# Pairs of row blocks in the last fold, one-row copies on ScalarE, even columns in the given order, and another order of the first blocks, in a spectral filter mixed with a token MLP

## The chip, the core and the metric

The kernel runs on one core of a Trainium2 chip. The metric is device time in microseconds: the median of three runs. Beside these runs, one execution was recorded by the hardware profiler, and all durations of single instructions come from that one. PE is the matrix engine, DVE the vector engine, ACT the scalar (activation) engine, POOL the GpSimd engine, and SP the engine that issues most of the DMAs. "L690" means line 690 of the kernel before.

## What is computed

The input `x` is 2048 rows of 512 bf16 numbers. Two branches are computed from it and mixed row by row with a gate:

```python
def _A_ref(x, w_r, w_i):            # spectral filter
    X = rfft2(x.astype(float32), axes=(-2, -1))
    X = X * (w_r + 1j * w_i)        # 2048 x 257 complex weights
    return irfft2(X, s=(S, D)).astype(bfloat16)

def _B_ref(x, w1, b1, w2, b2):      # MLP over the tokens
    h = _layernorm(x)               # over the 512 columns
    u = gelu(einsum("bsd,sf->bdf", h, w1) + b1)
    y = einsum("bdf,fs->bds", u, w2) + b2
    return y.transpose(0, 2, 1)

g = sigmoid((x * gate_w).sum(-1, keepdims=True))
return g * _A_ref(...) + (1 - g) * _B_ref(...)
```

The MLP has 2048 x 1792 weights each way. Both branches are matmuls in bf16: the transforms are products with tables of cosines and sines, split by radix-4 butterflies on DVE.

## The kernel before, in words

**Rows.** The 2048 rows are held as 16 blocks of 128. Block `j = 4q + r` is the rows `512q + 4a + r`, with `a` the partition. So `r` (0 to 3) is the row number modulo 4, and `q` the quarter.

**The MLP branch.** Layer norm of block `j`: `bn_stats` and `bn_aggr` on DVE (L471, L472), or for the blocks in `ASTAT` a sum and a sum of squares on ACT (L481, L485, into a shared scratch in `gl`); the root on ACT (L475); then either a reciprocal and a normalization on DVE (L495, L496, for the blocks in `OWN`) or a reciprocal and a product on DVE (L518, L519) and the normalization on ACT (L522). The first product (`m1`, L690) sums over all 16 blocks for each of 14 column tiles `ft` of `w1`: 224 matmuls of 512 columns. The first six tiles use the weights `wa`, block after block in the order `jorder`, as blocks become ready; the other eight use `wb` and need a free PSUM bank `acc`, which the GELU of an earlier tile frees (ACT, L704; a table load stands ahead of the first). The second product (`m2`, L966) makes one row block of the output from 14 matmuls. ACT (L986) scales it by `1 - g` into the output buffer; for the last two blocks DVE does it (L1004) with the addition.

**The filter branch.** For each `r`: butterflies over the quarters (`q4a`, `q4b`: L530, L531, L536, L537) give `xf`; PE transforms the rows (`fa`, four tasks per `r`, L547 to L550, table `ta`) into PSUM, with the even frequencies `0, 2, 4, ...` interleaved from two products, each written with a stride of two; ACT casts to `X` (L553); DVE does the first butterflies over the columns (`d4a`, `d4b`: L560 to L567). Then follow radix-4 butterflies over `r` (L586 to L599), the column transform (`fb`, L655 to L658) with casts to `B` (L662), the product with the filter on DVE (L805 to L831), the inverse butterflies, the inverse row transform (`i1`, L874 to L881) with casts (L887, L889) and folds (L897 to L910), and the inverse column transform (`i3`, L948 to L952). ACT scales its result by the gate into `eo` (L957). DVE folds `eo` (L971 to L975) and adds it to the output buffer (L992), block by block. Groups of blocks are stored by DMA.

**The filter's weights.** The filter needs each weight row and its mirror. The mirrored rows are loaded to `wt` and turned by a product with a permutation `flip` (`wf`, L742, cast at L746). A few rows that lie on no partition of their own are loaded to a strip (`wz`) and copied on partition 0 by five instructions of POOL per component (`special`, L445 to L449; components are the real and the imaginary part).

**The gate.** DVE multiplies `x` by `gate_w` (L715, four instructions, due number 6), ACT sums each block (L720, due number 5, 16 instructions); a tanh follows (L722) and DVE forms `g` and `1 - g`.

**The order.** Every piece of work is a task with an engine, an estimated duration, a due number (`prio`, a smaller one is more urgent), the tasks that it depends on, and buffers that it takes and frees. `Plan.order` simulates the engines with these estimates: whenever an engine is free it takes the most urgent task that is ready, a filler of low urgency too. Tasks are emitted in that order, and on the chip each engine runs its list strictly in order. A step on one engine depends on its predecessor on the same engine with a latency of 0.1 us in the plan. Loads are tasks of SP (or, for the first few, of ACT), with an estimate of their landing from bytes and packets. Loads that are issued before 6 us of the plan are counted 1.35 times as long.

Of the kernel before, what the change touches and what calls it, by code (L numbers as in the profile page):

```python
# [35 lines left out]
def make_tables():  # L36
# [10 lines left out]
    for r in range(4):  # L47
# [82 lines left out]
    flip = np.concatenate([np.eye(P)[::-1], np.eye(P)[(P - p) % P]], 1)  # L130
# [7 lines left out]
class Plan:  # L138
# [32 lines left out]
    def order(self):  # L171
# [17 lines left out]
        while events:  # L189
# [16 lines left out]
            while progress:  # L206
                progress = False
                for eng, ts in pending.items():
# [15 lines left out]
                    if best.pk:  # L224
# [4 lines left out]
                        dma_free = max(dma_free, issue + 0.8) + work / 16 * (1.35 if issue < 6.0 else 1.0)  # L229
# [25 lines left out]
def act(n, ptr=0):  # L255
    return 0.065 + 0.09 * ptr + n / 1200.0
# [12 lines left out]
def kernel(  # L269
# [25 lines left out]
    NEO, NES = 4, 2  # L295
# [49 lines left out]
    a0 = add("SP", 0.01, alloc_first, writes=["warm", "xs", "eps"], prio=-9)  # L345
# [34 lines left out]
    def ld_x0(q, eng, prio):  # L380
        ld([("x", 0, q)], lambda q=q: t["x"][:, q, 0, :], x4[:, q, 0, :], (P, 1024), prio, eng)
# [49 lines left out]
    def ld_W(comp, pr):  # L431
        v = wsrc[comp].rearrange("(e c k) l -> c e k l", e=4, k=4)
        z = wsrc[comp].rearrange("(e h q k) l -> h k q e l", e=4, h=2, k=2)
# [9 lines left out]
        def special():  # L443
            G, W, u, w = nc.gpsimd, t["W"], t["wt"], wz()
            G.tensor_copy(u[0:1, comp, 0, 0:2, 0:257], w[:, 5:8:2, 0:257])  # L445
            G.tensor_copy(u[0:1, comp, 0, 2, 0:257], w[:, 6, 0:257])
            G.tensor_copy(u[0:1, comp, 0, 3, 0:257], w[:, 0, 0:257])
            G.tensor_copy(W[0:1, comp, 0, 2:4, 0, 0:257], w[:, 1:4:2, 0:257])
            G.tensor_copy(t["wn"][:, comp, 0:257], w[:, 4, 0:257])  # L449
        add("POOL", 7.0, special, reads=[(k, comp) for k in ("wz", "u0", "u1", "w0", "w1")], writes=[("W", comp), ("wt", comp)], prio=0)  # L450
# [12 lines left out]
    OWN = {0: (0, 4, 8, 12), 1: (1, 5), 2: (2,), 3: ()}  # L463
    ASTAT = (8, 12, 5)
    QS, DP = 0.2, 4.9
    for r in range(4):
# [10 lines left out]
        for n, j in enumerate(OWN[r]):  # L477
            pj = 0.1 * n + ((-2.0, -2.0, -2.0, -1.8)[n] if r == 0 else 1.2 * r + 0.2 * n)
            if j in ASTAT:
# [7 lines left out]
                add("ACT", 0.6, asum, reads=[("x", r, j // 4)], writes=[("mvs", j), "ascr"], prio=-2 + 0.1 * n)  # L487
                add("ACT", 0.6, asq, reads=[("x", r, j // 4), ("mvs", j)], writes=[("mv", j), "ascr"], prio=-2 + 0.1 * n)
            else:
                add("DVE", 0.82, lambda j=j: stat(j), reads=[("x", r, j // 4)], writes=[("mv", j)], prio=pj)  # L490
            add("ACT", 0.28, lambda j=j: sq(t["rstd"][:, j:j + 1], t["mv"][:, j, 1:2], 1.0 / D if j in ASTAT else 1.0),
                reads=[("mv", j), "eps"], writes=[("rstd", j)], prio=-3)

# [4 lines left out]
            add("DVE", 0.55, nh, reads=[("mv", j), ("x", r, j // 4)], writes=[("rstd", j), ("h", j)], prio=pj - 0.05)  # L498
# [39 lines left out]
        pq = -1.75 if r == 0 else 1.2 * r + 1.2 + QS  # L538
# [3 lines left out]
        for dq in range(4):  # L542
            def fa(r=r, dq=dq):
# [3 lines left out]
                T.matmul(pa[:, 0, :, 0:P:2], lhsT=w(0), rhs=ta[:, 0:128], start=True, stop=True)  # L547
                T.matmul(pa[:, 0, :, 1:P:2], lhsT=w(1), rhs=ta[:, 128:256], start=True, stop=True)  # L548
# [123 lines left out]
    bt = add("PE", 0.3, biasT, reads=["b1", "b2", "flip"], writes=["pbias"], prio=10.096, alloc=["fa"])  # L672
# [7 lines left out]
    jorder = [4 * q + r for r in range(4) for q in range(4)]  # L680
# [32 lines left out]
    for r in range(4):  # L713
# [4 lines left out]
        for q in range(4):  # L718
            def ga(q=q, r=r):
                A.activation(t["x"][:, q, r, :], t["x"][:, q, r, :], ActF.Copy, accum_out=t["glog"][:, 4 * q + r:4 * q + r + 1])  # L720
            gates.append(add("ACT", act(512) + 0.1, ga, reads=xk, writes=[("xg", q, r)], prio=5))
# [217 lines left out]
    for grp in groups:  # L939
        for j in grp:  # L940
# [17 lines left out]
            add("ACT", act(512, 1), i3ev, reads=[("i3", j), "g"], writes=[("eo", j)], prio=1.5, alloc=["eo"], free=[tag])  # L958
# [11 lines left out]
            def fold(e, o, s):  # L970
                V.tensor_copy(s[:, :, :, 0], e[:, :, 0:129:128].rearrange("p h k -> p k h"))  # L971
# [4 lines left out]
            tfold = tiny(1) + 4 * tt(256)  # L976
            quart = lambda v: v.rearrange("p h (k d) -> p (h k) d", k=2)

            if j < LATE:
                def es(j=j, fold=fold, quart=quart):  # L980
                    s = sb([P, 2, 2, P], BF16, "es", NES)
                    fold(t["eo", j], quart(t["eo", j][:]), s)
                add("DVE", tfold, es, reads=[], writes=[("eo", j)], prio=4, alloc=["es"], free=["es"])

# [3 lines left out]
                add("ACT", act(512, 2), yev, reads=[("y", j, 0), "omg"], writes=[("o", j)], prio=1, free=["acc"], after=gates)  # L988

                def fin(j=j):  # L990
                    o = tbuf(j)
                    V.tensor_add(o, o, t["eo", j][:])  # L992
                add("DVE", tt(512), fin, reads=[("eo", j)], writes=[("o", j)], prio=4, free=["eo"])
            else:
                def es(j=j, fold=fold, quart=quart):
                    e, s = t["eo", j], sb([P, 2, 2, P], BF16, "es", NES)
                    V.tensor_scalar_add(e[:, 0, 0:129], e[:, 0, 0:129], t["ombb2"][:, j:j + 1])
                    fold(e, quart(tbuf(j)), s)
                add("DVE", tfold + 0.15, es, reads=[("eo", j), "omg"], writes=[("o", j)], prio=4, alloc=["es"], free=["eo", "es"], after=gates)
# [49 lines left out]
```

## Time and profile before

| what | value |
|---|---|
| median of three runs | 137.5 us (137.49 to 137.58) |
| the profiled execution | 137.48 us, of which its span is 135.6 us |
| granted PE clock in it | 0.993 |
| start of the first product (L690) on PE | 6.55 us |
| POOL's copies | 29.25 to 33.1 us and 38.78 to 43.1 us |
| DVE, 30 to 50 us | 9.93 us busy of each 10 |
| ACT, 30 to 40, 40 to 50, 50 to 60 us | 9.93, 9.68, 9.49 us busy |
| ACT, 70 to 80, 80 to 90 us | 1.46, 3.36 us busy |
| DMA engines | over 0.98 busy from 5 to 50 us, 328 to 388 GB/s |

The span runs from the first to the last instruction or transfer of the execution; the difference to its time lies around it. "Busy" counts what the profiler records of an instruction. The records of consecutive instructions overlap on an engine, so the distance between starts, not the recorded length, is what one costs in a stream. Idle time is put down to the instruction that released it.

### The profile page before, as it was taken

The page shows a single profiled execution, that of the slowest core. Times are in us where ns is not written, and L with a number is a line of the kernel's source. Part 1 is how long each engine was busy: PE and PEld are TensorE (multiplying, and loading weights), DVE is VectorE, ACT ScalarE, POOL GpSimd, SP SyncE. Part 2 cuts the span into 40 slices and gives each one's busy share as a digit, 9 for nine tenths or more (in the row PEclk, how much of TensorE's full clock was granted, in tenths as well). Part 3 has the DMA queues.
Part 4 walks back from the last instruction along what each step waited for, and adds up shares of the span by engine and source line. Part 5 has one row for each costly group of instructions (what it writes and reads, how often), then busy time and mean ns, then how long its engine had stood idle before and what let it go on. Part 6 is the DMA issues. An engine that isn't in the chain of part 4 may idle for free.

```text
span 135.6 us, 2193 instructions
## 1 busy us (share of the span) xinstructions
PE 127.0 (94%) x771; PEld 72.2 (53%) x771; DVE 118.1 (87%) x301; ACT 84.8 (63%) x175; POOL 8.4 (6%) x14
## 2 busy tenths in 40 slices
PE   6499999999999999999999899999999999999970
PEld 2146564654645457564445445555776575665660
DVE  2799989899999999819999999999659779999990
ACT  2976686699999999898111063222699377656400
POOL 0000000037057000000000000000000000000000
PEclk9999999999999999999999999999999999999997
DMA  4999999999999960980006900000000000321322
GB/s 119 342 342 369 355 374 348 336 299 344 332 324 405 407 267 0 286 337 0 0 0 221 400 0 0 7 0 2 0 0 0 5 0 0 155 114 48 155 77 80
DMA packets 17151, 23.22 MB, mean 171 GB/s; under 512 B 976, under 2 KB 14580, under 8 KB 17140
## 3 DMA queue, kind: packets, MB, share of 16 engines
q1 hardware_dynamic: 16564, 22.46, 48.8%
q10 hardware_dynamic: 576, 0.62, 1.5%
q8 instruction: 6, 0.10, 0.3%
q14 instruction: 5, 0.04, 0.1%
HBM read 20.97 MB, written 2.10 MB: 170 GB/s over the span
## 4 chain that ended last, share of the span: by engine, by line
PE 48%; DVE 36%; ACT 4%; DMA 4%; issue 3%; ACTq 1%; DVEq 0%
PE acc L966 19%; PE acc L690 16%; DMA wb<-in_B_w_dram 4%; PE fb L690 4%; DVE x L992 3%; DVE eo L974 3%; DVE es L973 3%; DVE st L560 2%; DVE X L561 2%; DVE es L972 2%; DVE eo L975 2%; DVE x L715 2%; DVE st L587 2%; DVE xp L586 2%; DVE X L567 2%
## 5 line engine op out<-in xcount | busy, mean ns | idle before, releaser
L966 PE MATMUL acc<-gl,wb 128*128 128x512 bf16 (+1 forms) x128 | 31.1, 373 | 0.4 <-DMA wb<-in_B_w_dram 0.4
L690 PE MATMUL acc<-h,wb 128*128 128x512 bf16 x128 | 30.0, 379 | 0.0
L986 ACT ACTIVATE x<-acc,ombb,omg 128x512 bf16<-128x512 f32 x14 | 10.8, 778 | 22.0 <-PE acc L966 22.0
L966 PE MATMUL acc<-gl,wa 128*128 128x512 bf16 (+1 forms) x96 | 24.2, 372 | 0.0
L966 PEld LDWEIGHTS <-wb 128*128 128x128 bf16 x136 | 14.8, 114 | 11.0 <-DMA wb<-in_B_w_dram 1.1
L690 PEld LDWEIGHTS <-wb 128*128 128x128 bf16 x128 | 12.5, 98 | 12.8
L690 PE MATMUL acc<-h,wa 128*128 128x512 bf16 x64 | 16.9, 379 | 1.9 <-DVE h L496 1.9
L966 PEld LDWEIGHTS <-wa 128*128 128x128 bf16 x102 | 11.4, 114 | 8.2
L690 PEld LDWEIGHTS <-wa 128*128 128x128 bf16 x96 | 9.4, 98 | 11.4 <-issue 1.8
L704 ACT ACTIVATE gl<-acc,b1f 128x512 bf16<-128x512 f32 x12 | 8.0, 694 | 6.1 <-PE acc L690 6.1
L553 ACT CAST X<-fa 128x512 bf16<-128x512 f32 x16 | 9.1, 586 | 2.9 <-PE fa L550 2.9
L471 DVE BATCH_NORM_STATS2 stats<-x 128x6 f32<-128x512 bf16 x13 | 8.8, 679 | 1.8 <-DMA x<-in_A_x_dram 1.7
L720 ACT ACTIVATE x<-x 128x512 bf16<-128x512 bf16 x16 | 10.0, 647 | 0.0
L690 PE MATMUL fb<-h,wa 128*128 128x512 bf16 x32 | 9.8, 379 | 0.0
L522 ACT ACTIVATE h<-x,nmr,rstd 128x512 bf16<-128x512 bf16 x9 | 7.1, 809 | 1.5 <-DVE nmr L519 1.5
L957 ACT ACTIVATE eo<-fa,g 128x512 bf16<-128x512 f32 x8 | 5.5, 685 | 2.7 <-DVE x L992 2.7
L957 ACT ACTIVATE eo<-fb,g 128x512 bf16<-128x512 f32 x8 | 5.5, 684 | 0.0
L662 ACT CAST B<-fa 128x512 bf16<-128x512 f32 x8 | 4.9, 618 | 0.8 <-PE fa L658 0.8
L992 DVE TENSOR_TENSOR x<-x,eo 128x512 bf16<-128x512 bf16 x14 | 5.3, 417 | 0.0
L715 DVE TENSOR_TENSOR x<-x,gw 128x2048 bf16<-128x2048 bf16 x4 | 5.2, 1312 | 0.0
L548 PE MATMUL fa<-rot,gl 128*128 128x128 bf16 x16 | 5.0, 312 | 0.1
L662 ACT CAST B<-fb 128x512 bf16<-128x512 f32 x8 | 5.0, 629 | 0.0
(177 smaller groups left out, 252.6 us busy)
## 6 DMA issues: line engine op xcount, KB each, us to landing
wb<-in_B_w_dram SPq DMA_DIRECT2D x8, 512.0 KB, 6.9
wb<-in_B_w_dram SPq DMA_DIRECT2D x4, 1024.0 KB, 6.1
wa<-in_B_w_dram SPq DMA_DIRECT2D x3, 1024.0 KB, 12.0
wa<-in_B_w_dram SPq DMA_DIRECT2D x2, 768.0 KB, 8.4
out_dram<-x SPq DMA_DIRECT2D x3, 512.0 KB, 2.6
x<-in_A_x_dram SPq DMA_DIRECT2D x2, 512.0 KB
wa<-in_B_w_dram SPq DMA_DIRECT2D x2, 384.0 KB
rot<-dft_ti SPq DMA_DIRECT2D x1, 736.5 KB
```

Source lines behind the costliest of these rows:

```text
L471: V.bn_stats(out=t["stats"][:, j, :], in_=t["x"][:, j // 4, j % 4, :])
L522: add("ACT", act(512, 2), lambda j=j: A.activation(t["h"][:, j // 4, j % 4, :], t["x"][:, j // 4, j % 4, :], ActF.Identity, bias=t["nmr"][ ...
L553: add("ACT", act(512), lambda r=r, dq=dq: A.copy(t["X"][:, :, r, :, dq, :], t["pa", r, dq][:]), reads=[("pa", r, dq)], writes=[("X", r, dq ...
L662: A.copy(t["B"][:, lt, e, 2 * c:2 * c + 2, :].rearrange("p s (i b) -> p s i b", b=4), t["pb", lt, e, c][:].rearrange("p s b i -> p s i b"))
L690: T.matmul(t["u", ft][:], lhsT=w[:, j // 4, j % 4, c * P:(c + 1) * P], rhs=t["h"][:, j // 4, j % 4, :], start=(j == jorder[0]), stop=(j == ...
L704: gelus.append(add("ACT", act(512, 1), lambda ft=ft: A.activation(t["gl"][:, ft, :], t["u", ft][:], ActF.Gelu_apprx_tanh, bias=t["b1f"][:, ...
L715: add("DVE", tt(2048), lambda r=r: V.tensor_mul(t["x"][:, :, r, :], t["x"][:, :, r, :], t["gw"][:, None, :].to_broadcast([P, 4, D])), read ...
L720: A.activation(t["x"][:, q, r, :], t["x"][:, q, r, :], ActF.Copy, accum_out=t["glog"][:, 4 * q + r:4 * q + r + 1])
L957: A.activation(t["eo", j][:], t["i3", j][:], ActF.Copy, scale=t["g"][:, j:j + 1])
L966: T.matmul(t["y", j, n][:, cs], lhsT=w[:, o, 512 * q + r:512 * q + 512:4], rhs=t["gl"][:, ft, cs], start=(ft == 0), stop=(ft == NFT - 1))
L986: A.activation(tbuf(j).rearrange("p h d -> p (h d)"), t["y", j, 0][:], ActF.Identity, bias=t["ombb2"][:, j:j + 1], scale=t["omg"][:, j:j + 1])
L992: V.tensor_add(o, o, t["eo", j][:])
```

## The change

The change has these parts.

- **Fold in pairs.** `eo` holds two blocks (two such buffers for four single ones). For the first 14 blocks, the fold (five instructions) and the addition to the output act on two blocks each. The last two blocks are folded singly as before.
- **One-row copies.** The five copies per component go from POOL to ACT, with due number 4.5. The two loads that held rows of the even frequencies, `u0` and `w0`, become four loads of 64 partitions each (`u0`, `u2`, `w0`, `w2`), four more loads in all.
- **Even columns.** The two products of L547 and L548 write 64 columns each, one after the other, in place of interleaved columns. The tables, `flip` and the loads of the filter follow that order.
- **First blocks.** `r = 0` goes through its blocks in the order 0, 8, 4, 12. The squares of block 8 on ACT wait for block 0's root; the statistics of block 4 on DVE wait for block 0's normalization. The table `ta` of `r = 0` is loaded by SP, after `w1`'s third piece, in place of ACT.
- **Numbers of the plan.** `QS` (the due number of the quarters' butterflies for `r > 0`) goes from 0.2 to -0.2, early loads are counted 1.2 times as long in place of 1.35, and some estimates of ACT grow.

```diff
-        k = 2 * p
+        k = 4 * (p % 64) + 2 * (p // 64)
...
-            sg = alt[:, None]
+            sg = np.where(p < 64, 1.0, -1.0)[:, None]
...
-    flip = np.concatenate([np.eye(P)[::-1], np.eye(P)[(P - p) % P]], 1)
+    flip = np.concatenate([np.eye(P)[::-1], np.eye(P)[np.where(p < 64, (64 - p) % 64, 191 - p)]], 1)
...
-                        dma_free = max(dma_free, issue + 0.8) + work / 16 * (1.35 if issue < 6.0 else 1.0)
+                        dma_free = max(dma_free, issue + 0.8) + work / 16 * (1.2 if issue < 6.0 else 1.0)
...
-    return 0.065 + 0.09 * ptr + n / 1200.0
+    return 0.11 + 0.09 * ptr + n / 1200.0
...
-    NEO, NES = 4, 2
+    NEO, NES = 2, 2
...
-    a0 = add("SP", 0.01, alloc_first, writes=["warm", "xs", "eps"], prio=-9)
+    a0 = add("SP", 0.6, alloc_first, writes=["warm", "xs", "eps"], prio=-9)
...
+    ld_w10(2, "SP", -8.8)
     ld_x0(3, "ACT", -8.8)
-    ld_ta(0, -8.78, "ACT")
-    ld_w10(2, "SP", -8.8)
     ld_w10(1, "SP", -8.7)
+    ld_ta(0, -8.65)
     ld_w10(3, "SP", -8.6)
...
-                ("u0", lambda: t["wt"][:, comp, 0, :, 0:257], z[1, 0], (512, 514)),
+                ("u0", lambda: t["wt"][0:64, comp, 0, :, 0:257], z[0, 1, 0], (256, 514)),
+                ("u2", lambda: t["wt"][64:128, comp, 0, :, 0:257], z[1, 1, 0], (256, 514)),
...
-                ("w0", lambda: t["W"][:, comp, 0, :, 0, 0:257], z[0, 0], (512, 514)),
+                ("w0", lambda: t["W"][0:64, comp, 0, :, 0, 0:257], z[0, 0, 0], (256, 514)),
+                ("w2", lambda: t["W"][64:128, comp, 0, :, 0, 0:257], z[1, 0, 0], (256, 514)),
...
-            G, W, u, w = nc.gpsimd, t["W"], t["wt"], wz()
-            G.tensor_copy(u[0:1, comp, 0, 0:2, 0:257], w[:, 5:8:2, 0:257])
...
-        add("POOL", 7.0, special, reads=[(k, comp) for k in ("wz", "u0", "u1", "w0", "w1")], writes=[("W", comp), ("wt", comp)], prio=0)
+            W, u, w = t["W"], t["wt"], wz()
+            A.copy(u[0:1, comp, 0, 0:2, 0:257], w[:, 5:8:2, 0:257])
...
+        add("ACT", 2.2, special, reads=[(k, comp) for k in ("wz", "u0", "u1", "u2", "w0", "w1", "w2")], writes=[("W", comp), ("wt", comp)], prio=4.5)
...
-    OWN = {0: (0, 4, 8, 12), 1: (1, 5), 2: (2,), 3: ()}
+    OWN = {0: (0, 8, 4, 12), 1: (1, 5), 2: (2,), 3: ()}
...
-    QS, DP = 0.2, 4.9
+    QS, DP = -0.2, 4.9
...
-            pj = 0.1 * n + ((-2.0, -2.0, -2.0, -1.8)[n] if r == 0 else 1.2 * r + 0.2 * n)
+            pj = (-2.0, -1.95, -1.9, -1.62)[n] if r == 0 else 1.2 * r + 0.3 * n
...
-                add("DVE", 0.82, lambda j=j: stat(j), reads=[("x", r, j // 4)], writes=[("mv", j)], prio=pj)
+                add("DVE", 0.82, lambda j=j: stat(j), reads=[("x", r, j // 4)], writes=[("mv", j)], prio=pj, after=[n0] if j == 4 else ())
...
+            if j == 0:
+                s0 = sj
+            if j == 8:
+                aq.deps.add(s0)
...
-        pq = -1.75 if r == 0 else 1.2 * r + 1.2 + QS
+        pq = -1.65 if r == 0 else 1.2 * r + 1.2 + QS
...
-                T.matmul(pa[:, 0, :, 0:P:2], lhsT=w(0), rhs=ta[:, 0:128], start=True, stop=True)
-                T.matmul(pa[:, 0, :, 1:P:2], lhsT=w(1), rhs=ta[:, 128:256], start=True, stop=True)
+                T.matmul(pa[:, 0, :, 0:64], lhsT=w(0), rhs=ta[:, 0:128], start=True, stop=True)
+                T.matmul(pa[:, 0, :, 64:P], lhsT=w(1), rhs=ta[:, 128:256], start=True, stop=True)
...
-    jorder = [4 * q + r for r in range(4) for q in range(4)]
+    jorder = [4 * q + r for r in range(4) for q in ((0, 2, 1, 3) if r == 0 else range(4))]
...
-                t["eo", j] = sb([P, 2, L], BF16, "eo", NEO)
-                A.activation(t["eo", j][:], t["i3", j][:], ActF.Copy, scale=t["g"][:, j:j + 1])
+                if j % 2 == 0:
+                    t["eo", j // 2] = sb([P, 2, 2, L], BF16, "eo", NEO)
+                A.activation(t["eo", j // 2][:, j % 2], t["i3", j][:], ActF.Copy, scale=t["g"][:, j:j + 1])
...
-                V.tensor_add(o[:, 0:4:3], s[:, :, 0], s[:, :, 1])
-                V.tensor_sub(o[:, 2:0:-1], s[:, :, 0], s[:, :, 1])
+                sv = s.rearrange("p k (j h) d -> p j h k d", h=2)
+                for u in range(o.shape[1]) if o.shape[1] == 1 else (slice(None),):
+                    V.tensor_add(o[:, u, 0:4:3], sv[:, u, 0], sv[:, u, 1])
+                    V.tensor_sub(o[:, u, 2:0:-1], sv[:, u, 0], sv[:, u, 1])
...
+                if j % 2 == 0:
+                    continue
...
+                def es(j=j, fold=fold, quart=quart):
+                    s, e = sb([P, 2, 4, P], BF16, "es", NES)[:], t["eo", j // 2]
+                    fold(e[:].rearrange("p j h d -> p (j h) d"), quart(e[:]), s)
+                add("DVE", tiny(1) + 4 * tt(512), es, reads=[], writes=[("eo", j - 1), ("eo", j)], prio=4, alloc=["es"], free=["es"])
 
                 def fin(j=j):
-                    o = tbuf(j)
-                    V.tensor_add(o, o, t["eo", j][:])
-                add("DVE", tt(512), fin, reads=[("eo", j)], writes=[("o", j)], prio=4, free=["eo"])
+                    tbuf(j)
+                    o = t["tb_"][:, j - 1:j + 1]
+                    V.tensor_add(o, o, t["eo", j // 2][:])
+                add("DVE", tt(1024), fin, reads=[("eo", j - 1), ("eo", j)], writes=[("o", j - 1), ("o", j)], prio=4, free=["eo"])
```

More of the change, by code (lines that the diff above doesn't have):

```diff
@@ L432, in ld_W @@
         v = wsrc[comp].rearrange("(e c k) l -> c e k l", e=4, k=4)
-        z = wsrc[comp].rearrange("(e h q k) l -> h k q e l", e=4, h=2, k=2)
+        z = wsrc[comp].rearrange("(e h i n k) l -> n h k i e l", e=4, h=2, n=2, k=2)
         wz = lambda: t["xp"][0:1, 2048 + 8 * WL * comp:2048 + 8 * WL * (comp + 1)].rearrange("p (j l) -> p j l", j=8)
@@ L497, in nh @@
                                 t["rstd"][:, j:j + 1], op0=Alu.add if j in ASTAT else Alu.subtract, op1=Alu.mult)
-            add("DVE", 0.55, nh, reads=[("mv", j), ("x", r, j // 4)], writes=[("rstd", j), ("h", j)], prio=pj - 0.05)
+            nj = add("DVE", 0.55, nh, reads=[("mv", j), ("x", r, j // 4)], writes=[("rstd", j), ("h", j)], prio=pj - 0.05)
+            if j == 0:
+                n0 = nj
         rest = [j for j in range(r, NJ, 4) if j not in OWN[r]]
@@ L720, in ga @@
                 A.activation(t["x"][:, q, r, :], t["x"][:, q, r, :], ActF.Copy, accum_out=t["glog"][:, 4 * q + r:4 * q + r + 1])
-            gates.append(add("ACT", act(512) + 0.1, ga, reads=xk, writes=[("xg", q, r)], prio=5))
+            gates.append(add("ACT", 0.72, ga, reads=xk, writes=[("xg", q, r)], prio=5))
     add("ACT", 0.3, lambda: A.activation(t["g"][:], t["glog"][:], ActF.Tanh, scale=0.5),
@@ L955, in i3ev @@
             def i3ev(j=j):
-                t["eo", j] = sb([P, 2, L], BF16, "eo", NEO)
-                A.activation(t["eo", j][:], t["i3", j][:], ActF.Copy, scale=t["g"][:, j:j + 1])
-            add("ACT", act(512, 1), i3ev, reads=[("i3", j), "g"], writes=[("eo", j)], prio=1.5, alloc=["eo"], free=[tag])
+                if j % 2 == 0:
+                    t["eo", j // 2] = sb([P, 2, 2, L], BF16, "eo", NEO)
+                A.activation(t["eo", j // 2][:, j % 2], t["i3", j][:], ActF.Copy, scale=t["g"][:, j:j + 1])
+            i3e = add("ACT", act(512, 1), i3ev, reads=[("i3", j), "g"], writes=[("eo", j)], prio=1.5, alloc=["eo"] if j % 2 == 0 else (), free=[tag],
+                      after=[i3e] if j % 2 else ())
             parts = [slice(0, D)] if j < NJ - 1 else [slice(0, L), slice(L, D)]
```

31 lines of the change are left out of this document (13 added, 18 removed).

## The prediction, made before the changed kernel ran

> **What bounds the kernel now.** I read the page first, then the chain of waits, then the timelines of PE, DVE, ACT and POOL, stage by stage. The page shows who is full:
>
> ```profile
> PE 127.0 (94%) x771; PEld 72.2 (53%) x771; DVE 118.1 (87%) x301; ACT 84.8 (63%) x175; POOL 8.4 (6%) x14
> PE 48%; DVE 36%; ACT 4%; DMA 4%; issue 3%; ACTq 1%; DVEq 0%
> ```
>
> PE has 94% of the span, and the chain runs over PE and DVE in turn. The PE timeline says more than the share: from its first product at 6.55 to its last at 131.21 it stands still for only about 1.4 us (0.27 at 48.99, 0.21 at 55.91, 0.36 at 75.98, the rest at 34 and 96.5). So the kernel is PE's list of matmuls, plus what lies ahead of 6.55, plus what follows 131.21. The second is set by a queue on ACT:
>
> ```profile
> 4.85 0.72 ACT L485 ACTIVATE gl<-x,mv 128x512 f32<-128x512 bf16 x1
> 5.48 0.19 ACT L485 ACTIVATION_READ_ACCUMULATOR gl<-x,mv 128x1 f32 x1
> 5.57 0.65 ACT L475 ACTIVATE rstd<-mv,eps 128x1 f32<-128x1 f32 x3
> 6.08 0.41 DVE L496 TENSOR_SCALAR h<-x,mv,rstd 128x512 bf16<-128x512 bf16 x1
> 6.55 1.02 PE L690 MATMUL acc<-h,wa 128*128 128x512 bf16 x4 [1.91 <-DVE h L496]
> ```
>
> Columns: start, us, engine and line. Block 0's statistics were complete at 4.36 (L472, 4.18 plus 0.18), but its root (L475) stands on ACT behind the squares of block 8 and starts at 5.57. The third part, the end:
>
> ```profile
> 130.17 1.04 PE L966 MATMUL fa<-gl,wb 128*128 128x256 bf16 x8
> 130.72 1.13 DVE L1004 SCALAR_TENSOR_TENSOR x<-acc,omg,x 128x512 bf16<-128x512 f32 x2
> 131.78 0.47 DVE L1004 SCALAR_TENSOR_TENSOR x<-fa,omg,x 128x256 bf16<-128x256 f32 x1
> ```
>
> The last product ends at 131.21, its addition starts at 131.78: DVE is 0.57 late, since it folds without a pause from 109.33 on. From 131.78 to the end of the span (0.47 and a store) lie 3.8 us, which stay.
>
> **The row transform (fa).** The change's edit to L547 and L548 is priced by two tasks of the same shape, one writing PSUM with stride two, one writing runs of 64:
>
> ```profile
> 10.22 0.27 PE L547 MATMUL fa<-rot,gl 128*128 128x128 bf16 x1
> 10.28 0.31 PE L548 MATMUL fa<-rot,gl 128*128 128x128 bf16 x1
> 10.39 0.31 PE L549 MATMUL fa<-rot,gl 128*128 128x256 bf16 x1
> 10.54 0.27 PE L550 MATMUL fa<-rot,gl 128*128 128x256 bf16 x1
> 10.65 0.27 PE L547 MATMUL fa<-rot,gl 128*128 128x128 bf16 x1
> ...
> 50.00 0.22 PE L655 MATMUL fb<-tb,X 128*128 128x128 bf16 x1
> 50.05 0.22 PE L656 MATMUL fb<-tb,X 128*128 128x128 bf16 x1
> 50.11 0.38 PE L658 MATMUL fb<-tb,X 128*128 128x256 bf16 x2
> 50.33 0.22 PE L655 MATMUL fa<-tb,X 128*128 128x128 bf16 x1
> ```
>
> Start to start the first takes 0.43, the second 0.33, each with two products of 128 columns and two of 256. The stride is the visible difference. There are 16 such tasks: 16 x 0.10 = **-1.6 us of PE** (bounds 0, if something else makes L547 slow, and -1.75, at 0.11 each).
>
> **The start.** ACT issues three loads in place of four (0.48 less, so the table load starts at 2.14, not 2.62), sums block 8 (0.70) and then does block 0's root before the squares. Its statistics, at 4.36, then decide: root at about 4.45, reciprocal 0.31 later as now (5.57 to 5.88), and 0.67 from reciprocal to PE as now (5.88 to 6.55): PE starts at 5.43, **-1.1 us** (bounds 0 and -1.3). Its weights are there: PE's weight load saw them at 4.65. Behind the waiting squares of block 8 stand the sums of block 12 and, on DVE, block 8's h. That h is ready at about 6.9 (squares end 5.6, root 5.9, DVE has block 4's statistics until 6.3), and PE asks for it at 5.43 + 6 x 0.22 = 6.75; block 4's h comes at 7.5 and is asked for at 8.2. The new wait of block 4's statistics for block 0's h is covered the same way. The table of the row transform goes to SP as its fifth load, ahead of the last quarter of weights; PE used the table at 10.22 and that quarter later than 9, both some 2 us after such a load lands.
>
> **What is given back.** PE gains 1.1 + 12 x 0.10 = 2.3 us by the time it has the first three quarters of the transform done, but h comes from DVE and ACT, which start no earlier. The tightest place is the last block:
>
> ```profile
> 29.60 0.82 ACT L522 ACTIVATE h<-x,nmr,rstd 128x512 bf16<-128x512 bf16 x1
> 30.44 1.28 ACT L704 ACT_TABLE_LOAD   x1
> 31.73 2.42 ACT L704 ACTIVATE gl<-acc,b1f 128x512 bf16<-128x512 f32 x4
> ```
>
> Its h ends at 30.42, the first bank is free at some 32.4, and PE starts the next column tiles at 32.67: 0.3 in hand. If these times stay, PE keeps only 0.2 us plus what it can do while it waits: the transform of the fourth quarter, now at 34.05 to 37.11 (4 x 0.43 and 0.34 of waiting). The new offset QS places that quarter's butterflies ahead of d4 (L560 to L567 at 27.47 to 30.16, 2.7 us), so its matmuls are there from about 29.5; and the third quarter's casts leave ACT earlier, so block 15's h may come 0.5 to 1 sooner. Bounds for what PE keeps of 2.75 us: 0.6 (gate unmoved, transform where it is: 0.2 and 4 x 0.10) and 2.75. I take **2.05**, 0.7 given back, nearer the upper end since both moves are in the code.
>
> **The tail.** A pair of blocks takes DVE 2.68 us now (L972 at 109.51 and 112.19 in the chain). Joined: the small copy 0.09, four operations of 512 elements at 0.34 (three steps from L899 to L903, 98.49 to 99.50) and the addition of 1024 at 0.60 (L591 to L592): 2.05 and some gaps, 2.1. Seven pairs save 4.1. DVE then ends its folds at 130.80 - 4.1 = 126.7 even if it starts no earlier, and PE ends at 131.21 - 2.05 = 129.16. So PE is the bound there by 2.5 us, and of the 0.57 a gap as between L671's end (24.59) and L675 (24.63) is left: **-0.5 us** (bounds 0 and -0.55).
>
> **The one-row copies.** On POOL they cost DVE time: while they run (29.25 to 33.1, 38.78 to 43.1) L567 takes 0.83 in place of 0.41, L560 1.10 and 0.88 in place of 0.68, L715 1.41 in place of 1.21. Adding these starts up, DVE loses about 2.7 us. On ACT no row shows them; between L755 (16 elements, 0.27) and L553 (512, 0.59) lie 0.4 for 257 elements and 0.6 for 514, so 2.4 us per component, bounds 1.4 and 2.9. ACT is full from 30 to 60, but 13 of the 16 gate sums (L720, 0.61 each) stand there with less urgent priority and need only be done by 79.23, where L986 first uses their result; ACT idles 22.0 us after 63. So on the path: 0. Without that cover it is 2.4 us on a cast of B. The 2.7 us of DVE is not counted either, PE being the bound; it is a reserve. Four more loads make SP later by 0.9 each; behind them stand the second wb load (used near 52, landed by 38) and w2, which waits 14.0 for PE anyway: 0. L715 fills DVE's pauses as before: 0.
>
> **The sum**: 137.48 (the profiled execution; 135.6 of span and 1.9 around it, the median being 137.5) - 2.05 - 0.5 = **134.9 us**.
>
> **Rivals.** *The gate holds.* PE keeps 0.6 of its lead: 137.48 - 0.6 - 0.5 = 136.4. For it: the 0.3 in hand, ACT and DVE full from 26 to 35. Against: the moved butterflies.
> *ACT waits for the filter.* Its queue is in order. If the copies stand ahead of h of block 7 (27.06), where ACT still has pauses, they wait for the rows (29.25 by POOL's start) and take 2.4; ACT goes on at 31.7 instead of 27.06, all behind it, the last h and the first bank, 4.6 later. PE fills 2.1 with the fourth quarter and had 0.3: 2.2 net on top of the lead lost, 137.48 + 2.2 - 0.5 = 139.2. It decides against the kernel when the block delays ACT by more than 2.9. Against it: the plan released L742 for 42.51 after 7 us booked for the copies, so it expects the rows after 32, later than they come, and ACT is then busy with more urgent work. The Trainium skill (SBUF — State Buffer, "Can I just issue two DMAs to hit both halves?") says that a transfer to 64 partitions reaches half the ports and that two of them serialize. The split loads would then take twice as long, an estimate from that page of 1.5 us more per component. No run here shows it; it would make this rival likelier and touch nothing else.
> *The plan shuffles away the gain.* Waits at the four places where PE stands still now grow by 2.5: 137.5.
>
> **Chances.** Forecast 0.70 (its own range 133.4 to 135.8), gate 0.16, ACT wait 0.08, shuffle 0.04, still faster than 133.4 by fewer waits 0.02. The low end is 137.48 - 2.75 - 0.55 - 0.8 (the three waits gone) = 133.4; the high end, 136.8, takes in the gate with 0.4 for a longer wait there. Some 0.2% (0.3 us) is what can be told from no change: faster 0.88, same 0.04, slower 0.08.
>
> **What would show it.** PE's first L690 near 5.4; the fa tasks at 0.33 each; no POOL copies and L567 at 0.41 throughout; a stop of PE of under 1 us between 28 and 33; folds in pairs of 2.1; the last addition within 0.1 of PE's end at about 129. A PE start after 6.2, fa tasks still at 0.43, or an ACT wait on the filter's loads ahead of the first L704 would prove the forecast wrong.

## The result, and the profile after

| | before | after |
|---|---|---|
| median of the runs | 137.5 us (137.46 to 137.58) | 135.7 us (135.34 to 136.38) |
| profiled execution; its span | 137.48; 135.6 | 136.38; 134.5 |
| first product of the MLP starts (L690, now L699) | 6.55 | 5.33 |
| last product of PE ends | 131.21 | 128.54 |
| first fold starts on DVE | 109.33 | 109.81 |
| last addition starts on DVE | 131.78 | 130.72 |

The ratio is 0.9875, 95% interval 0.9833 to 0.9916: faster by some 1.25%. The forecast was 134.9. The recorded execution is the slowest of its four, so what follows explains 136.38 and not the median. The table holds the main point: PE is done 2.67 us earlier, the last addition comes only 1.06 us earlier, and 1.06 is close to what the time lost (137.48 to 136.38, 1.1). Lines have moved: L690 is now L699, L966 is L977, L971 to L975 are L982 to L988, L992 is L1007, L1004 is L1019, L662 is L671.

The page of the changed kernel, busy times and the chain's shares:

```profile
PE 124.2 (92%) x758; PEld 70.9 (53%) x771; DVE 112.4 (84%) x259; ACT 88.9 (66%) x185; POOL 0.2 (0%) x4
...
PE 42%; DMA 28%; DVE 13%; SPq 8%; ACT 4%; issue 2%; DVEq 0%; ACTq 0%
```

PE has 2.8 us less work, DVE 5.7 less, ACT 4.1 more. DMA, which had 4% of the chain, has 28%. Most of that are loads of the MLP's weights and of the gate's row; 6% is the load of the filter's `w_i` rows into `W`, which ACT's copy at 45.16 (below) waits for. The start, in the timeline of all engines:

```profile
4.34 0.29 ACT L477 ACTIVATE rstd<-mv,eps 128x1 f32<-128x1 f32 x1
4.54 0.70 ACT L487 ACTIVATE gl<-x,mv 128x512 f32<-128x512 bf16 x1
...
4.87 0.41 DVE L503 TENSOR_SCALAR h<-x,mv,rstd 128x512 bf16<-128x512 bf16 x1
...
5.33 1.02 PE L699 MATMUL acc<-h,wa 128*128 128x512 bf16 x4 [0.59 <-DVE h L503]
```

Block 0's root now stands ahead of the squares of block 8. In PE's timeline, one row transform and the stops of over 0.25 us that come after the start (a row's time is where the stop ends):

```profile
8.37 1.02 PE L699 MATMUL acc<-h,wa 128*128 128x512 bf16 x4 [0.27 <-DVE h L503]
...
9.66 0.22 PE L556 MATMUL fa<-rot,gl 128*128 128x128 bf16 x1
...
9.99 0.22 PE L556 MATMUL fa<-rot,gl 128*128 128x128 bf16 x1
...
32.84 0.81 PE L699 MATMUL acc<-h,wb 128*128 128x512 bf16 x3 [0.38 <-ACT gl L713]
...
47.19 0.20 PE L761 MATMUL fa<-wt,flip 128*128 128x8 bf16 x2 [1.00 <-ACT W L755]
```

A task of the transform takes 0.33 (9.66 to 9.99). The stop at the first GELU bank (32.84) is 0.38. The largest stop, 1.00 up to 47.19, comes from ACT, whose timeline shows the one-row copies of the second component:

```profile
43.27 0.40 ACT L449 COPY wt<-xp 1x257 bf16<-1x257 bf16 x1
45.16 0.62 ACT L450 COPY W<-xp 1x514 bf16<-1x514 bf16 x1 [1.49 <-DMA W<-in_A_w_i_dram]
45.69 0.40 ACT L451 COPY wn<-xp 1x257 bf16<-1x257 bf16 x1
```

Five copies cost some 2.0 us a component, and here ACT also stands 1.49 us for a load: the rows of `w_i` in `W` landed near 45.1. In the kernel before POOL could start on all five copies at 38.78. The tables by stage show why, first of the kernel before, then of the one after (after the window: us, PE, PE loads, DVE, ACT, POOL, clock, busy share of the DMA engines, GB/s):

```profile
25.00:30.00 5.00, 5.00 (x32) 3.00 (x30) 4.38 (x14) 4.39 (x10) 0.75 (x2) 1.00 1.16 307
...
40.00:45.00 5.00, 5.00 (x29) 2.67 (x28) 4.93 (x8) 5.00 (x14) 3.10 (x3) 1.00 1.03 402
```

```profile
25.00:30.00 5.00, 5.00 (x30) 2.57 (x28) 4.72 (x15) 4.06 (x9) 0.00 (x0) 1.00 1.17 219
...
40.00:45.00 5.00, 5.00 (x25) 2.29 (x24) 4.90 (x17) 3.52 (x8) 0.00 (x0) 1.00 1.23 202
```

The DMA engines are at least as busy as before, and move 219 and 202 GB/s in place of 307 and 402 in two stretches in which the loads of 64 partitions run. Between them, from 35 to 40 us, such loads run too, and the rate is 298 in place of 314. The Trainium skill (SBUF — State Buffer, "Can I just issue two DMAs to hit both halves?") says that a pair of such transfers serializes, and that only one transfer over all 128 partitions reaches all the ports. The trace agrees in that the rate falls; no run here shows the ports.

The end, in the timeline of all engines:

```profile
127.50 1.04 PE L977 MATMUL fa<-gl,wb 128*128 128x256 bf16 x8
...
129.92 0.28 DVE L988 TENSOR_TENSOR x<-es 128x256 bf16<-128x256 bf16 x1
130.32 0.48 DVE L1019 SCALAR_TENSOR_TENSOR x<-acc,omg,x 128x256 bf16<-128x256 f32 x1
130.72 0.48 DVE L1019 SCALAR_TENSOR_TENSOR x<-fa,omg,x 128x256 bf16<-128x256 f32 x1
```

PE ends at 128.54; DVE is still folding at 130.2 and adds the finished product 2.18 us late (0.57 before). So DVE's path sets the end, and it has two idle stretches. The first, in DVE's timeline:

```profile
54.83 0.17 DVE L808 TENSOR_TENSOR ce<-cm 128x8 f32<-128x8 f32 x1
60.09 0.17 DVE L785 CAST c<-B 128x8 f32<-128x8 bf16 x1 [5.08 <-ACT B L671]
...
60.66 1.22 DVE L814 TENSOR_TENSOR xp<-B 128x2048 bf16<-128x2048 bf16 x1
```

DVE arrives 2.7 us earlier than before (55.0 against 57.7) and waits 5.08 us (2.66 before) for the casts of the even half of `B`. The same wait in the kernel before, in DVE's timeline:

```profile
60.33 0.17 DVE L776 CAST c<-B 128x8 f32<-128x8 bf16 x1 [2.66 <-ACT B L662]
```

DVE takes that half first, and ACT casts it last: the odd half was complete at 53.65. DVE's work on that half thus starts at 60.66, against 60.91 before, and the first fold no earlier than before. The second idle stretch lies among the folds. The tables of the stage from the first fold to the last addition, before and after:

```profile
109.33:131.78 22.45, 21.87 (x158) 13.88 (x155) 21.82 (x99) 12.04 (x19) 0.00 (x0) 1.00 0.21 83
```

```profile
109.81:130.72 20.91, 18.62 (x138) 12.17 (x138) 18.76 (x57) 11.28 (x18) 0.00 (x0) 1.00 0.24 95
```

DVE's busy time fell by 3.06 (21.82 to 18.76), the stage by 1.54: idle time grew from 0.63 to 2.15. The waits of DVE and of ACT from 105 us on (us in total, times, longest):

```profile
DVE es L982 <- ACT eo L967: 4.3, 3, 2.7
```

```profile
ACT eo L967 <- DVE x L1007: 4.1, 4, 2.1
```

The longest of DVE's three waits, 2.7, ends with the first fold and so lies ahead of the stage; the other two, 0.79 each, lie in it. Each engine waits for the other. `eo` has two buffers, of two blocks each; a buffer comes free only when both its blocks are added, and the next fold needs both of its blocks there.

### The profile page after: what moved, and what is told of

Its sections match the earlier page's. It is cut to its first block, busy times and chain, and to the rows that moved or that the text cites. A ratio compares the mean times of both kernels' runs of the same rounds, so it can differ in the third digit from the quotient of the medians.

```text
span 134.5 us, 2134 instructions
## 1 busy us (share of the span) xinstructions
PE 124.2 (92%) x758; PEld 70.9 (53%) x771; DVE 112.4 (84%) x259; ACT 88.9 (66%) x185; POOL 0.2 (0%) x4
## 4 chain that ended last, share of the span: by engine, by line
PE 42%; DMA 28%; DVE 13%; SPq 8%; ACT 4%; issue 2%; DVEq 0%; ACTq 0%
PE acc L977 21%; PE acc L699 12%; DMA wa<-in_B_w_dram 9%; SPq L310 8%; DMA gw<-in_gate_w_dram 8%; DMA W<-in_A_w_i_dram 6%; DMA wb<-in_B_w_dram 4%; ACT eo L967 3%; DVE eo L987 2%; DVE es L984 2%; DVE x L1007 2%; DVE es L983 2%; DVE eo L988 2%; PE fb L883 1%; PE fb L667 1%
## 5 line engine op out<-in xcount | busy, mean ns | idle before, releaser
L977 PE MATMUL acc<-gl,wb 128*128 128x512 bf16 (+1 forms) x124 | 30.8, 372 | 0.2
L699 PE MATMUL acc<-h,wb 128*128 128x512 bf16 x124 | 28.6, 379 | 0.5 <-ACT gl L713 0.4
L977 PE MATMUL acc<-gl,wa 128*128 128x512 bf16 (+1 forms) x94 | 23.9, 372 | 0.1
L977 PEld LDWEIGHTS <-wb 128*128 128x128 bf16 x136 | 15.1, 114 | 10.7 <-DMA wb<-in_B_w_dram 0.8
L699 PEld LDWEIGHTS <-wb 128*128 128x128 bf16 x128 | 12.5, 98 | 14.0 <-DMA W<-in_A_w_r_dram 0.7
L699 PE MATMUL acc<-h,wa 128*128 128x512 bf16 x61 | 16.9, 379 | 1.0 <-DVE h L503 0.9
L977 PEld LDWEIGHTS <-wa 128*128 128x128 bf16 x102 | 11.3, 114 | 8.0 <-issue 0.2
L699 PEld LDWEIGHTS <-wa 128*128 128x128 bf16 x96 | 9.3, 98 | 9.9 <-issue 1.2
L699 PE MATMUL fb<-h,wa 128*128 128x512 bf16 x32 | 9.4, 379 | 0.0
L982 DVE COPY es<-eo 128x8 bf16<-128x8 bf16 (+1 forms) x9 | 1.6, 182 | 4.4 <-ACT eo L967 4.3
L477 ACT ACTIVATE rstd<-mv,eps 128x1 f32<-128x1 f32 x16 | 4.7, 296 | 0.5 <-DVE rstd L527 0.4
L671 ACT CAST B<-fa 128x512 bf16<-128x512 f32 x8 | 4.8, 598 | 0.3 <-PE fa L667 0.3
L671 ACT CAST B<-fb 128x512 bf16<-128x512 f32 x8 | 4.8, 601 | 0.0
```

Source lines behind the costliest of these rows:

```text
L671: A.copy(t["B"][:, lt, e, 2 * c:2 * c + 2, :].rearrange("p s (i b) -> p s i b", b=4), t["pb", lt, e, c][:].rearrange("p s b i -> p s i b"))
L699: T.matmul(t["u", ft][:], lhsT=w[:, j // 4, j % 4, c * P:(c + 1) * P], rhs=t["h"][:, j // 4, j % 4, :], start=(j == jorder[0]), stop=(j == ...
L977: T.matmul(t["y", j, n][:, cs], lhsT=w[:, o, 512 * q + r:512 * q + 512:4], rhs=t["gl"][:, ft, cs], start=(ft == 0), stop=(ft == NFT - 1))
```

## The experiments

All times are medians. The runs of a1 to b1, of the c's and of the d's were made on three chips, each time beside runs of the kernel before on the same chip, whose median was 137.58 to 137.65. The ratio to these, with its 95% interval, is formed from the runs and is not the quotient of the medians. "Changed kernel" is the one after. Times of single instructions come from one recorded execution of each kernel.

**a1_single_folds.** The changed kernel with the old folds, one block at a time, and four buffers.

```diff
-    NEO, NES = 2, 2
+    NEO, NES = 4, 2
...
-                t["eo", j // 2] = sb([P, 2, 2, L], BF16, "eo", NEO)
+                t["eo", j] = sb([P, 2, L], BF16, "eo", NEO)
...
-                add("DVE", tiny(1) + 4 * tt(512), es, reads=[], writes=[("eo", j - 1), ("eo", j)], prio=4, alloc=["es"], free=["es"])
+                add("DVE", tfold, es, reads=[], writes=[("eo", j)], prio=4, alloc=["es"], free=["es"])
```

> The changed kernel with the last fold and the addition undone to one block per instruction and four single buffers; all else as changed (135.7 us). Theory (the pairs brought little: with two pair buffers DVE and ACT wait for each other, 5.2 us for two pairs against 5.36 for four single blocks before): 135.5 to 136.3, DVE without pauses from the first fold to the last. Rival (the pairs carry much of the gain, 4.1 us of DVE time being saved at the end): 137 or more.

Measured: 138.21 us (137.17 to 139.23), ratio 0.9999 (0.995 to 1.0048). PE's last product ends at 128.72, the last addition starts at 131.76, where it started before. The rival held: PE's 2.5 us alone are worth nothing, and without the pairs the change shows no gain.

**a2_copies_on_pool.** The one-row copies back on POOL.

```diff
-            A.copy(u[0:1, comp, 0, 0:2, 0:257], w[:, 5:8:2, 0:257])
+            nc.gpsimd.tensor_copy(u[0:1, comp, 0, 0:2, 0:257], w[:, 5:8:2, 0:257])
...
-        add("ACT", 2.2, special,
+        add("POOL", 7.0, special,
```

> The changed kernel with the ten one-row copies back on POOL. Theory (the wait of ACT for the second component's rows, 1.49 us in the profile, costs PE 1.0 us and delays B, and it is this that scatters the runs over 1 us): ACT has no such wait and the runs scatter less; but POOL takes back up to 2.7 us of DVE time ahead of B, so 135 to 136. Rival (the copies on ACT are free and DVE's time counts): 136.5 or more. The rows would still land at about 45, so the turning products still wait for them.

Measured: 137.55 us (137.09 to 138.03), ratio 0.9957 (0.9916 to 0.9998). The last addition starts at 132.22, 1.50 later than in the changed kernel, and PE stops for 1.65 us up to 49.09, for DVE's `X`. POOL's copies of the second component start at 44.00 and not at 38.78 as before, beside the split loads, which are still there. The rival held here too: DVE's loss, set down as a reserve, counts. What POOL's copies cost with whole loads, this run doesn't show.

**a3_whole_loads_stride_two.** Row transform, tables and loads of the filter as before the change: the stride of two and whole loads.

```diff
-                ("u0", lambda: t["wt"][0:64, comp, 0, :, 0:257], z[0, 1, 0], (256, 514)),
-                ("u2", lambda: t["wt"][64:128, comp, 0, :, 0:257], z[1, 1, 0], (256, 514)),
+                ("u0", lambda: t["wt"][:, comp, 0, :, 0:257], z[1, 0], (512, 514)),
...
-                T.matmul(pa[:, 0, :, 0:64], lhsT=w(0), rhs=ta[:, 0:128], start=True, stop=True)
+                T.matmul(pa[:, 0, :, 0:P:2], lhsT=w(0), rhs=ta[:, 0:128], start=True, stop=True)
```

> The changed kernel with the even columns as before (products written with a stride of two, loads of 128 partitions, old tables). Theory (loads to 64 partitions run at half the rate): the second component's rows land at 38 to 41 and not at 45, ACT does not wait for them, PE does not stop at 47; the row transform takes 0.43 a task again, 1.7 us more of PE. Net 135.5 to 136.5 with a scatter of under 0.4. Rival (the split loads cost nothing, the lateness has another cause): rows still at 44 to 45, and 137 or more.

Measured: 136.23 us (136.1 to 137.12), ratio 0.9876 (0.9807 to 0.9945): no difference from the changed kernel that these intervals could show. PE's last product ends at 128.66 (128.54) and the last addition starts at 130.84 (130.72). ACT does not wait in the copies and PE does not stop near 47. What the runs of 64 columns give PE, the split loads that come with them take back. In this kernel the DMA engines move 301 GB/s from 25 to 30 us and 390 from 40 to 45, which ties the loss of rate to the split (c3, with the split loads, moves 240 and 265). Its runs lie 1.0 us apart, where under 0.4 was expected, so the split loads are not all that scatters the runs.

**b1_interleave_in_cast.** Both at once: a3 with runs of 64 columns in PSUM, interleaved by ACT's cast, so that the loads stay whole. (The cast turns the odd columns too; the table `ta` holds these in an order that makes up for it.)

```diff
-                T.matmul(pa[:, 0, :, 0:P:2], lhsT=w(0), rhs=ta[:, 0:128], start=True, stop=True)
+                T.matmul(pa[:, 0, :, 0:64], lhsT=w(0), rhs=ta[:, 0:128], start=True, stop=True)
...
-lambda r=r, dq=dq: A.copy(t["X"][:, :, r, :, dq, :], t["pa", r, dq][:]),
+lambda r=r, dq=dq: A.copy(t["X"][:, :, r, :, dq, :].rearrange("p l c (i n) -> p l c i n", n=2), t["pa", r, dq][:].rearrange("p l c (n i) -> p l c i n", n=2)),
```

> As the run with whole loads, but the two products are written one after the other and ACT's cast to X puts the even columns in order (it reads PSUM in pairs of columns 64 apart). Loads of 128 partitions, copies on ACT. Theory (stride costs PE 1.65 us, split loads cost about 1 us): 134.0 to 135.0, row transform 0.33 a task, rows at 38 to 41, scatter under 0.4, faster than both the changed kernel and the one with the stride. Rival (the end hangs on DVE's fold and not on PE): within 0.4 of the run with the stride. Should the cast slow down by the strided reading, its 16 instructions show it (0.58 now).

Measured: 135.67 us (135.44 to 135.77), ratio 0.9819 (0.9757 to 0.9881). PE's last product ends at 128.07, the last addition starts at 130.25, 2.18 later, as in the changed kernel and in a3: DVE is the bound, as the rival had it. But the time meets neither forecast: it is 0.56 below that of a3, where the rival said within 0.4, and above the range of the theory. Against a3 PE ends 0.59 earlier (not 1.65: it came to its full rate later, see the last section, and stops 0.37 at the first GELU bank, where a3's does not), the even half of `B` is complete some 0.5 earlier, the first fold starts 0.59 earlier (109.34 and 109.93), and so does the last addition. What PE gains ahead of `B` does reach the end here, through the casts that DVE waits for.

**c1_swap_halves, c4_before_swap.** DVE takes the odd half of `B` first, which ACT has cast first: in the changed kernel (c1) and in the kernel before (c4).

```diff
-    for lt in range(2):
-        pr = 3.2 + 0.1 * lt
+    for lt in (1, 0):
+        pr = 3.3 - 0.1 * lt
```

> The changed kernel with one loop turned round: the filter product takes the odd half (lt = 1) before the even one. Nothing else. Theory (the end hangs on DVE's path, not on PE: DVE stands still for 5.08 us at 55 to 60 because the even half of B, which it takes first, is cast last, though the odd half lies ready): the pause shrinks to under 1 us, the last fold starts 4 us earlier, near 105.5, DVE's folds end ahead of PE, and the end follows PE's last product (128.5) by some 4 us: 134.2 for the profiled execution, 133.5 to 134.5 in the median, against 135.7. Rival (PE is the bound already, the 2.2 us between PE's end and the last addition are the work of the last two blocks): within 0.4 of the changed kernel.

> The kernel before with only the loop turned round. Theory (two bounds lay almost level before: PE ends at 131.2, DVE's folds let the last addition start at 131.78): DVE's pause of 2.66 us goes, the folds end ahead of PE, the end follows PE: 0.4 to 0.6 less, 136.9 to 137.2. Rival (DVE alone was the bound): 1.5 us or more less. Second rival (PE alone): nothing.

Measured: c1 134.16 us (132.85 to 135.16), ratio 0.9686 (0.9593 to 0.9779); c4 136.77 us (136.48 to 138.02), ratio 0.9926 (0.9881 to 0.9972). In c1 the work on `B` starts at 56.67, the first fold at 106.90 (109.81), and the last addition starts 0.03 after PE's end, at 130.35. The recorded execution took 135.16, 1.0 over the median: ACT waited 2.2 us for the `w_i` rows and PE 2.25 us. In c4 the first fold is at 106.80, 2.53 earlier, and the last addition 0.04 after PE's end (132.56). The swap takes DVE off the path in both. In the kernel before DVE was only 0.57 late, so PE, the other bound, lets little of the 2.53 through; the time came out somewhat below the theory's. The recorded execution of c4 took 138.02, and its PE ends 1.35 later than in the kernel before, since it came late to its full rate (last section); it shows which engine waits, and the median what the swap is worth.

**c2_interleave_and_swap, c3_three_pair_buffers.** b1 with the swap (c2); the changed kernel with a third buffer for the pairs, and one for the folded sums to make room (c3):

```diff
-    NEO, NES = 2, 2
+    NEO, NES = 3, 1
```

> Whole loads, contiguous products, even columns put in order by the cast, and the loop turned round as in the run before it. Theory: PE's last product ends at 128.1, as without the turned loop, and the end is 0.1 + 3.8 behind it: 133.3 to 134.0, faster than every kernel so far and steadier. Rival (another wait takes over once the pause is gone, the single row that goes through DRAM-side loads and PE ahead of the inverse transform): 134.5 to 135.5.

> The changed kernel with three buffers for pairs in place of two (and one scratch of the fold in place of two, to make room). Theory (two buffers make ACT and DVE wait for each other, 4.1 us and 1.6 us of pauses in the fold phase): from the first fold to the last addition 19.0 to 19.6 in place of 20.9, 134.3 to 135.0. Rival (the pauses of ACT are only where it has nothing to do, since PE's i3 products are placed late by the plan): 20.5 or more, no change.

Measured: c2 133.87 us (133.44 to 133.94), ratio 0.969 (0.9622 to 0.9757), the last addition 0.03 after PE's end. c3 134.33 us (133.93 to 134.5, and one run of 139.01), ratio 0.9721 (0.9616 to 0.9826). The table of c3's fold stage:

```profile
109.07:128.47 19.40, 18.49 (x140) 12.18 (x138) 18.68 (x57) 11.17 (x18) 0.00 (x0) 1.00 0.24 96
```

DVE has the same work as in the changed kernel (18.68 and 18.76) in 1.5 us less; the last addition comes 0.35 after PE's end. So the mutual waits were the buffers' doing. The rest of c3's lead in this record is another thing: the `w_i` rows landed in time (copy L450 at 43.76, without a wait), PE does not stop near 47, the even half of `B` is ready 0.88 earlier (59.69 and 60.57) and the first fold starts 0.74 earlier than in the changed kernel.

**d3_old_start, d2_interleave_swap_old_start.** The old order of the first blocks and loads, with the estimates that went with it, in the changed kernel (d3), whose end hangs on DVE, and in c2 (d2), whose end hangs on PE.

```diff
-    OWN = {0: (0, 8, 4, 12), 1: (1, 5), 2: (2,), 3: ()}
+    OWN = {0: (0, 4, 8, 12), 1: (1, 5), 2: (2,), 3: ()}
...
-            if j == 8:
-                aq.deps.add(s0)
```

> The changed kernel with the old order of the first blocks, first loads and block 0's root and nothing else. Theory: its end hangs on DVE, which has a wait of 5.1 at B's even half: PE's last product ends near 129.7 (128.54 in the changed kernel), but the last addition starts at 130.4 to 131.0 (130.72), time 135.4 to 136.1. Rival: what starts earlier ends earlier: last addition near 131.8, time 136.6 to 137.0.

> The interleaving cast and the swapped halves, with the old order of the first blocks, first loads and block 0's root. Theory: PE is the bound there, so its start counts in full: first product of the MLP at 6.55, PE's last product near 129.7, last addition within 0.1 of it, time 134.8 to 135.2 (133.87 with the new start). Rival: the end hangs on DVE there too: 133.7 to 134.2.

Measured: d3 135.49 us (135.18 to 135.57), ratio 0.9817 (0.975 to 0.9883); PE starts at 6.54 and ends at 129.22, and the last addition starts at 130.51. The earlier start shows no gain in the changed kernel, as its theory had it. PE's lead of 1.21 is 0.68 at the end; the stops of 0.27 and 0.38 are not there in d3. The `w_i` rows come into it as well: ACT and PE wait for them in both records, they landed 0.34 earlier in d3 (copy L450 at 44.82), and the even half of `B` was ready 0.34 earlier (60.23). d2 134.17 us (134.14 to 135.8), ratio 0.9763 (0.9664 to 0.9863), 0.3 more than c2 and not the 1.1 of its theory. The time lies in the rival's range, but not for the rival's reason: the last addition starts 0.04 after PE's end (128.82). The two recorded executions differ in more than the start: c2's PE lost 0.8 us by coming late to its full rate (last section), and d2's stops 0.79 us up to 31.15 for a cast, where c2's stops 0.18. What the earlier start is worth where PE is the bound stays open.

**d4_swap_single_folds, d1_interleave_swap_three_buffers.** The two changes to the folds again where PE is the bound: a1 with the swap (d4), c2 with c3's buffers (d1). Their edits are those above.

> The changed kernel with the halves swapped and the old folds, one block at a time. Theory: the first fold comes near 107 and the folds take 22.5, so DVE is done at 129.5 to 130.3, level with PE: time 134.1 to 134.9, and the pairs, worth 2.5 without the swap, are worth at most 0.7 with it. Rival: the pairs are worth 2.5 wherever z comes: 136.4 to 136.9.

> The interleaving cast, the swapped halves and three pair buffers together (one buffer of the folded sums in place of two, for room). Theory: with the halves swapped PE is the bound at the end, so a shorter fold phase is worth nothing: PE's last product ends at 128.3 to 128.8 and the last addition starts within 0.1 of it, time 133.5 to 134.2, the same as with two buffers (133.87). Rival: the waits between DVE and ACT in the folds also hold PE back through the banks of the last products: PE's last product at 127.8 or earlier, time 132.5 to 133.2.

Measured: d4 133.13 us (132.62 to 134.06), ratio 0.9657 (0.9579 to 0.9735); d1 133.47 us (133.42 to 133.5), ratio 0.9674 (0.9609 to 0.9739). The end of d4, in the timeline of all engines:

```profile
126.80 1.04 PE L975 MATMUL fa<-gl,wb 128*128 128x256 bf16 x8
127.88 0.48 DVE L1013 SCALAR_TENSOR_TENSOR x<-fa,omg,x 128x256 bf16<-128x256 f32 x1 [1.04 <-PE fa L975]
```

DVE waits 1.04 us for PE there, with single folds; the first fold had started at 103.66. The forecast of 107 came from c1, whose record holds the wait of 2.2 us for the `w_i` rows; here that wait is 0.19. The time lies 1.0 under the theory's range. The pairs, without which the gain was nil in a1, bring nothing that shows once the halves are swapped, and in d1 the third buffer adds nothing that the intervals show. Both kernels beat the changed one and the one before.

## Why the prediction was right in part

**Right.** The start (5.43 forecast, 5.33), the row transform (0.33 a task), and what is given back at the gate: PE was to end at 129.16 and ended at 128.54, with a stop of 0.38 where under 1 was forecast. No POOL copy is left to slow DVE. The first rival, the gate, had the right place (the second set of column tiles starts at 32.84, 32.67 before) and too high a price. That the time fell into the range is in part luck: the forecast had the wrong engine at the end, and PE's term, which came to nothing, was made up in part by a tail that gave twice its forecast.

**The step that failed** is in the tail: "DVE then ends its folds at 130.80 - 4.1 = 126.7 even if it starts no earlier", and from it "PE is the bound there by 2.5 us". The folds ended at 130.2. The size of a pair was nearly right (two pairs and one wait of 0.79 take 5.18, from 117.25 to 122.43, so 2.19 each, 2.1 forecast, which makes 0.6 in seven pairs), but DVE's work in the stage fell by 3.06 and not 4.1, two buffers gave 1.52 of that back as mutual waits (c3 gets that back), and the first fold came 0.48 later, as it needs two blocks of `eo` where it needed one (109.29 with single folds in a1). Sum: 0.48 - 3.06 + 1.52 = -1.06, the shift of the last addition.

**What had been overlooked** is the wait for `B`, 2.66 us, which stood in the trace of before. All that DVE gained ahead of 60 us (no POOL beside it, an earlier PE) ran into it. The even half was complete only 0.26 earlier (DVE's second cast of it, 60.57, 60.83 before), and PE starts the first product of the inverse column transform at 108.03, against 108.13. So PE's lead, the largest term of the sum (2.05), was worth next to nothing at the end of the recorded execution, nor does a1 or d3 show a gain by it, and the tail (0.5) gave 1.06. Where no wait for a load lies in between (b1 against a3), PE's gain ahead of `B` does reach the end.

**The copies** were set at 0 on the path. The work on ACT was hidden (2.0 us a component against the estimate of 2.4), but taking them off POOL counts: 1.5 us of the end beside the split loads (a2). The four more loads were also set at 0, and are not: the rate falls while they run, and they hold ACT for 1.49 us and PE for 1.00. That is the second rival's mechanism, in the second component and not ahead of the first GELU; the prediction had named it and kept it out of the sum. The wait also holds up the casts of `B`, and so the end, by some 0.7: where it is missing (c3), the first fold starts 0.74 earlier. That is an estimate from two recorded executions, whose kernels differ only in the buffers of the folds.

**Open.** Why single runs of one kernel lie 1 us and more apart (the changed kernel 135.34 to 136.38, the kernel before 137.31 to 139.31 beside the experiments) was not settled. The landing of the `w_i` rows moves from one recorded execution to the next (copy L450 at 43.76 in c3, 43.96 in d4, 45.16 here, 46.91 in c1), and so does the moment at which PE comes to its full rate; either may have a part in it, but a3 and the kernel before, which have no split loads, scatter too. Only one execution of each kernel was recorded. Not tried: single folds and the swap with whole loads, and the copies elsewhere in ACT's order.

## What to carry to other kernels

An engine that is 94% busy and ends the chain is the bound only as long as the other branch isn't level with it: the addition that was 0.57 us late said that DVE's path was as long, and then an early wait on that path (2.66 us for `B`) swallows what is saved ahead of it. Where two halves of a buffer are made in one order and used in the other, look there first; the one loop turned round brought the first fold 2.5 us forward in the kernel before. It takes both bounds to move the end: in the kernel before the turned loop alone gave 0.7% (c4), what the change gives PE, without pairs or turned loop, nothing (a1), and both together 3.4% (d4). Joining two units per instruction also joins their buffers: count them anew, or the saved work comes back as waiting.

## What the runs showed of the hardware

PE comes to its full rate at a moment that differs from one recorded execution to the next, and the granted clock does not show it (1.00 from 4 to 8 us in both cases below). PE's timeline, in the changed kernel and in c2, the nine products that run ahead of the MLP and then the MLP's first four:

```profile
1.21 3.52 PE L360 MATMUL fa<-xp 128*128 128x512 bf16 x9 [1.21 <-DVE xp L321]
5.33 1.02 PE L699 MATMUL acc<-h,wa 128*128 128x512 bf16 x4 [0.59 <-DVE h L503]
6.19 0.59 PE L699 MATMUL fb<-h,wa 128*128 128x512 bf16 x2
```

```profile
1.21 4.02 PE L360 MATMUL fa<-xp 128*128 128x512 bf16 x9 [1.21 <-DVE xp L321]
5.41 1.82 PE L697 MATMUL acc<-h,wa 128*128 128x512 bf16 x4 [0.17 <-DVE h L501]
7.06 0.59 PE L697 MATMUL fb<-h,wa 128*128 128x512 bf16 x2
```

In the first, four products take 0.86 from start to start of what follows; in the second 1.65. The nine early products take longer there too (4.02 and 3.52), and PE lost 0.8 us. In six of the fourteen recorded executions the MLP's first products are slow and the nine take 4.02 (b1, c1, c2, c4, d1, d4); in the other eight the nine take 3.42 to 3.84. It happens with the old start as with the new. The loss isn't always the same: in c4 the first ten products take 4.12 from start to start, against 2.16 in the kernel before. The Trainium skill (TensorE: Matmul & The Clock Gate, "What's actually happening") has the rate decided in windows of some 3.4 us that run free of the kernel, so that the same kernel starts differently from run to run. The traces agree as far as they go (c1 differs from the changed kernel only in a loop that comes into play after 50 us, and starts the other way); no run here measures the window, and no kernel was recorded twice.
